# All attention ahead of the feed-forward: float32r scores on row halves, tails in quarters, the attention result kept in DRAM

## The chip, the core and the metric

The kernel runs on one core of one Trainium2 chip. A core has a matrix engine (TensorE, PE in the profile, with its weight loads listed apart as PEld), VectorE (DVE), ScalarE (ACT), GpSimd (POOL) and a queue processor (SyncE, SP) that issues transfers; POOL can issue transfers too. Each engine takes its instructions strictly in the order in which the program lists them and waits on semaphores. The metric is the device time of one execution in microseconds; less is better.

## What is computed

Sigmoid attention, and behind it a feed-forward layer with exact GELU, all in float32. Cut to what matters:

```python
q, k, v: (8, 12, 448, 64)            # batch, heads, tokens, head size
scores = q @ k.T / sqrt(64) - log(448)
x = sigmoid(scores) @ v              # laid out as (8*448 = 3584 tokens, 12*64 = 768)
h = x @ w_in                         # (768, 2048), float64 in memory
out = (0.5 * h * (1 + erf(h / sqrt(2)))) @ w_out      # (2048, 768), float64 in memory
```

There is no sum over keys in the sigmoid, so each score can be used as soon as it is there. The weights arrive as 64-bit floats, and the kernel itself makes 32-bit floats of them by integer operations ("decoding").

## The kernel before

**Two kinds of float32 product.** A float32 matmul of the source becomes two weight loads and two matrix instructions in the trace. A float32r matmul becomes one of each, but its operands carry fewer bits; where full precision is wanted, each operand is split into a float32r high part and the float32r rest, and three products (low x high, high x low, high x high) are added up in PSUM. The split is one copy on ScalarE and one subtraction on VectorE.

**The feed-forward** is written in float32r splits throughout: tokens are taken in blocks of 512, seven of them. `ffn1` (L433) makes 16 hidden tiles `ph` of 18 matmuls each (L428 to L430, six chunks of 128 channels times three products), applies GELU twice on ScalarE (L445, L446) and takes the difference on VectorE (L447). `ffn2` (L460) makes 6 output tiles `po` of 48 matmuls each (L477 to L479). So a block has 288 + 288 = 576 matmuls of 512 columns. Weights stream through `Weights`: a unit (16 "in", 12 "out") is loaded from a scratch copy in DRAM (`wst`), split into `whl` on ScalarE (L226) and VectorE (L227), and used.

**Decoding** comes first for each weight: `decoder` (L87) cuts the weights into 40 pieces (16 of 768 columns, 24 of 512), loads each as 64-bit words (`raw`, `raw_ring`, L110), and takes five VectorE and two ScalarE instructions for it (L117 to L147). What comes out is used directly for block 0 and stored in DRAM for the other blocks.

**Attention** is written in two ways. Three of the eight batches are "plain" (`scores_plain` L333, `values_plain` L349): scores and values are float32 matmuls, for two heads at once. The two heads of a pair lie on partitions 0 to 63 and 64 to 127 of `qr` and `kr`, so their score matmuls use the two row halves of the matrix engine, and the value matmuls use its two column halves. 448 keys are taken as four chunks of 128, of which the last overlaps the third by half; the overlapped rows of its probabilities are zero (`a_last`). Two plain batches run alone at the start (`attention_first` L398), 12 pairs, with the first pieces of decoding beside them, and the result goes to `xh` and `xl`. The third plain batch and the other five batches are woven into `ffn2` of the block ahead (`window` L490): a few attention instructions, then some feed-forward matmuls, and so on. The five later batches are written in float32r (`split_head`, `scores` L281, `values` L376): per head, 7 score matmuls and 7 value matmuls of 128 x 128 weights and 448 columns, with q, k, v and also the probabilities split into high and low parts. One batch (the plain one of `b == 0`) is cut into seven groups of 64 tokens through `scr_x`, and each block takes 448 tokens of one batch and 64 of that one.

What sets the order: nothing but the order in which the Python code calls the engines. `until(share)` in `window` spreads the attention evenly over a block's `ffn2`.

## Time and profile before

| what | value |
|---|---|
| median of three runs | 1220.3 us (1219.89 to 1221.09) |
| span of the profiled execution | 1224.1 us, 3.8 us over that median |
| busy share of PE, DVE, ACT, POOL | 99%, 63%, 67%, 1% |
| granted TensorE clock, mean | 0.998 |
| first score matmul, first feed-forward matmul | 4.10 us, 91.94 us |
| last block of the feed-forward, with no attention in it | 1089.72 to 1220.29 us |
| moved by DMA | 172.23 MB, mean 141 GB/s |

The span is the profiled execution's own time, from its first to its last instruction; the runs are timed apart from it. A busy share counts an instruction from its start to its modelled end, and matmuls overlap, so 99% for PE does not say that the engine had no more to give. Times within the trace count from the start of the span. "x16" in a row is a count of instructions, and the name in front of "<-" is what they write.

### The profile page before, as it was taken

What the parts mean: (1) busy time and instruction counts of PE and PEld (TensorE: products, weight loads), DVE (VectorE), ACT (ScalarE), POOL (GpSimd) and SP (SyncE); (2) the same over time, 40 slices, a digit from 0 to 9 for tenths busy, and PEclk for the clock granted to TensorE, in tenths of its full rate; (3) what the DMA queues carried; (4) which work ended last, traced back from release to release, by engine and by line L of the source; (5) the groups of instructions that cost most, each with busy time, mean ns of one, the idle gap of its engine ahead of it and who ended that gap; (6) DMA issues with size and microseconds to landing.
All of it is one profiled execution on the core that took longest, in us unless ns stands there. A gap on an engine that the chain in (4) does not pass through costs nothing.

```text
span 1224.1 us, 15057 instructions
## 1 busy us (share of the span) xinstructions
PE 1210.4 (99%) x5448; PEld 961.8 (79%) x5448; DVE 769.2 (63%) x1127; ACT 815.5 (67%) x1247; POOL 8.6 (1%) x18
## 2 busy tenths in 40 slices
PE   8999999999999999999999999999999999999998
PEld 4338866668888888888888888888888888888887
DVE  4777788623589734798445896447984378953420
ACT  7886576534699744899546997459984489954421
POOL 0000000000000000000000000000000000000000
PEclk9999999999999999999999999999999999999999
DMA  8994567524443135442244432345422544223330
GB/s 278 300 283 153 183 214 246 183 82 154 154 140 113 57 104 174 150 143 73 91 157 147 142 108 76 123 145 162 133 69 87 172 148 147 78 82 104 131 114 26
DMA packets 79881, 172.23 MB, mean 141 GB/s; under 512 B 24256, under 2 KB 39616, under 8 KB 79808
## 3 DMA queue, kind: packets, MB, share of 16 engines
q1 hardware_dynamic: 78080, 164.99, 42.4%
q0 software_dynamic: 1728, 6.29, 1.3%
q8 instruction: 43, 0.70, 0.2%
q14 instruction: 30, 0.25, 0.1%
HBM read 144.90 MB, written 26.35 MB: 140 GB/s over the span
## 4 chain that ended last, share of the span: by engine, by line
PE 95%; DMA 3%; DVE 1%; ACT 1%; SPq 0%; issue 0%; DVEq 0%; ACTq 0%
PE po L477 13%; PE po L478 13%; PE po L479 12%; PE ph L428 12%; PE ph L429 12%; PE ph L430 12%; PE pav L386 7%; PE sc L294 6%; PE pav L356 3%; PE sc L340 3%; DMA raw_ring<-w_in_dram 1%; PE sc_l L289 1%; DMA raw<-w_in_dram 1%; DMA qr<-q_dram 1%; DVE me_ring L117 0%; SPq L328 0%
## 5 line engine op out<-in xcount | busy, mean ns | idle before, releaser
L477 PE MATMUL po<-g,whl 128*128 128x512 f32 x672 | 263.3, 392 | 0.0
L478 PE MATMUL po<-g,whl 128*128 128x512 f32 x672 | 262.3, 390 | 0.0
L479 PE MATMUL po<-g,whl 128*128 128x512 f32 x672 | 261.9, 390 | 0.0
L428 PE MATMUL ph<-xh,whl 128*128 128x512 f32 x672 | 261.5, 389 | 0.0
L429 PE MATMUL ph<-xl,whl 128*128 128x512 f32 x672 | 261.4, 389 | 0.0
L430 PE MATMUL ph<-xh,whl 128*128 128x512 f32 x672 | 261.4, 389 | 0.0
L227 DVE TENSOR_TENSOR whl<-wst,whl 128x768 fp32r<-128x768 f32 (+1 forms) x168 | 179.6, 1072 | 65.1 <-ACT whl L226 61.9
L447 DVE TENSOR_TENSOR g<-gf,g 128x512 fp32r<-128x512 f32 x112 | 77.5, 692 | 212.0 <-ACT g L446 211.8
L445 ACT ACTIVATE gf<-ph 128x512 f32<-128x512 f32 x112 | 66.9, 597 | 199.4 <-PE ph L430 185.5
L226 ACT CAST whl<-wst 128x768 fp32r<-128x768 f32 (+1 forms) x168 | 155.4, 928 | 5.5 <-PE po L479 4.2
L477 PEld LDWEIGHTS po<-g,whl 128*128 128x128 f32 x672 | 126.2, 188 | 31.9 <-issue 8.1
L428 PEld LDWEIGHTS ph<-xh,whl 128*128 128x128 f32 x672 | 126.1, 188 | 26.9 <-issue 0.7
L479 PEld LDWEIGHTS po<-g,whl 128*128 128x128 f32 x672 | 126.1, 188 | 26.8
L430 PEld LDWEIGHTS ph<-xh,whl 128*128 128x128 f32 x672 | 126.1, 188 | 26.2
L429 PEld LDWEIGHTS ph<-xl,whl 128*128 128x128 f32 x672 | 126.1, 188 | 26.1
L478 PEld LDWEIGHTS po<-g,whl 128*128 128x128 f32 x672 | 126.2, 188 | 23.8
L314 ACT ACTIVATE a<-sc 128x896 f32<-128x896 f32 (+1 forms) x174 | 128.3, 786 | 17.3 <-PE sc L340 8.3
L308 DVE TENSOR_TENSOR al<-a,ah 128x896 fp32r<-128x896 f32 x120 | 97.8, 855 | 35.4 <-ACT ah L307 35.4
L307 ACT CAST ah<-a 128x896 fp32r<-128x896 f32 x120 | 85.7, 754 | 5.6 <-PE pav L386 4.2
L386 PE MATMUL pav<-ah,vs 128*128 128x448 f32 x240 | 87.7, 365 | 0.0
L294 PE MATMUL sc<-qs,ks 128*128 128x448 f32 x360 | 82.9, 366 | 0.0
L294 PEld LDWEIGHTS sc<-qs,ks 128*128 128x128 f32 x360 | 67.6, 188 | 6.8
(60 smaller groups left out, 1210.4 us busy)
## 6 DMA issues: line engine op xcount, KB each, us to landing
wst<-scr_in SPq DMA_DIRECT2D x96, 384.0 KB, 3.1
wst<-scr_out SPq DMA_DIRECT2D x72, 512.0 KB, 3.3
kr<-k_dram SPq DMA_DIRECT2D x30, 448.0 KB, 4.3
vr<-v_dram SPq DMA_DIRECT2D x48, 256.0 KB, 4.6
out_dram<-ob SPq DMA_DIRECT2D x42, 224.0 KB, 2.0
raw_ring<-w_in_dram SPq DMA_DIRECT2D x11, 768.0 KB, 7.0
raw_ring<-w_out_dram SPq DMA_DIRECT2D x16, 512.0 KB, 4.7
qr<-q_dram SPq DMA_DIRECT2D x36, 224.0 KB, 3.2
```

What stands on the lines that cost most here:

```text
L226: nc.scalar.copy(hl[:, 0, :w], t[:, :w])
L227: nc.vector.tensor_tensor(hl[:, 1, :w], t[:, :w], hl[:, 0, :w], op=ALU.subtract)
L294: nc.tensor.matmul(o, ks[:, keys], qs, start=n == 0, stop=n == 1)
L308: nc.vector.tensor_tensor(al[t][:, c], a[t][:, c], ah[t][:, c], op=ALU.subtract)
L314: nc.scalar.activation(a, sc, AF.Sigmoid, bias=NEG_LOG_S, scale=SCALE)
L386: nc.tensor.matmul(pav[:, :S], vs[:, j, c], a, start=n == 0, stop=n == len(terms) - 1)
L428: nc.tensor.matmul(ph, wl, xh[:, cc], start=cc == 0, stop=False)
L429: nc.tensor.matmul(ph, wh, xl[:, cc], start=False, stop=False)
L430: nc.tensor.matmul(ph, wh, xh[:, cc], start=False, stop=cc == NC - 1)
L477: nc.tensor.matmul(po, wl, g[fc][:, 0], start=first, stop=False)
L478: nc.tensor.matmul(po, wh, g[fc][:, 1], start=False, stop=False)
L479: nc.tensor.matmul(po, wh, g[fc][:, 0], start=False, stop=last)
```

## The change

**All attention is done first**, in one loop over 24 units (8 batches times 3); a unit is two pairs of heads, p = 0 and p = 1. There is no attention in the feed-forward any more, and no pair is woven into `ffn2`.

**Scores** (`scores`): for each pair and each of the three full chunks of 128 keys, q and k are split into `hi` and `lo` (`split`: the copy for p = 0 on ScalarE, for p = 1 on VectorE, both subtractions on VectorE), and three float32r products are added up, each for the two heads on the two row halves: 36 matmuls a unit. **The tail** of 64 keys is no longer an overlapped chunk: the tails of all four heads of a unit are four float32 matmuls of 64 x 64 weights, one on each quarter of the matrix engine (`QUARTERS`), and one sigmoid takes them all. **Values** stay float32 on column halves (`values`), 12 a unit, plus four quarters for the tail (`values_tail`). They are taken one unit later than the scores.

**The result** of a unit is copied from PSUM by VectorE and parked by POOL in `scr_x`, a DRAM buffer for all 3584 tokens, in float32 (`park`). Each block loads its 512 tokens from there (`load_x`) and splits them (`split_x`), in the middle of `ffn2` of the block ahead.

**Decoding** runs beside attention, one piece a unit up to 20 pieces (`AHEAD`), and the other 20 beside the first block. Every decoded unit is now stored to DRAM by POOL and loaded again, block 0 too. `raw` has three buffers of its own. Weights are split four units ahead everywhere.

The diff, cut to its core ("..." marks what is left out):

```diff
+    T = 512
+    NT = B * S // T
...
-    scr_x = tc.dram_tile([2, P, NPAIR, S], F32, name="scr_x")
+    scr_x = tc.dram_tile([P, NPAIR, B * S], F32, name="scr_x")
...
+    WHL, WST = 4, 3
...
-        raw_ring = sb.tile([P, 2, 2 * SUB], U32, tag="raw", name="raw_ring", bufs=1)
...
+                raw = sb.tile([P, 2 * SUB], U32, tag="raw", name=f"raw{i}", bufs=3)[:, : 2 * w]
...
+            if c0 + w == width(kind):
+                nc.gpsimd.dma_start(scratch(kind, u), self.out[:, : width(kind)])
+                self.done += 1
...
+        def to(self, chunks):
+            while self.taken < 1 + 2 * chunks:
+                next(self.steps, None)
+                self.taken += 1
...
+    AHEAD = 20
...
+                    dec.units(i + 1)
...
+            self.prepare_to(i + WHL)
...
-    def scores(b, h):
...
-            for n, lows in enumerate((0, S + TAIL)):
-                keys = slice(lows + c * P, lows + c * P + P)
-                nc.tensor.matmul(o, ks[:, keys], qs, start=n == 0, stop=n == 1)
...
+    def load_x(t):
+        nc.sync.dma_start(xl.bitcast(F32), scr_x[:, :, t * T : (t + 1) * T])
+    def split_x():
+        half = NPAIR // 2
+        for h in slice(0, half), slice(half, NPAIR):
+            nc.scalar.copy(xh[:, h], xl[:, h].bitcast(F32))
+            nc.vector.tensor_tensor(xl[:, h], xl[:, h].bitcast(F32), xh[:, h], op=ALU.subtract)
+    def attention(at, ps_sc, ps_av):
+        raws, vals, parts, probs, pavs, xs = {}, {}, {}, {}, {}, {}
+        total = B * NU
+        def load(u):
+            if u >= total:
+                return
+            b, n = divmod(u, NU)
+            raw = at.tile([P, 2, 2, S], F32, tag="qk", name=f"qk{u}", bufs=3)
+            pairs = (slice(0, 1), slice(1, 2)) if u == 0 else (slice(0, 2),)
+            for ps in pairs:
+                hps = slice(2 * n + ps.start, 2 * n + ps.stop)
+                nc.sync.dma_start(raw[:, ps, 0], q[b, hps].rearrange("p r s -> r p s"))
+                for j in range(2):
+                    src = k[b, hps, rows(j), j].rearrange("p r s -> r p s")
+                    nc.sync.dma_start(raw[rows(j), ps, 1], src)
+            raws[u] = raw
+        def load_v(u):
+            if u >= total:
+                return
+            b, n = divmod(u, NU)
+            vr = at.tile([P, 2, 2, FULL + 1, D], F32, tag="v", name=f"v{u}", bufs=3)
+            src = v[b, 2 * n : 2 * n + 2].rearrange("p r j c d -> r p j c d")
+            nc.sync.dma_start(vr, src)
+            vals[u] = vr
+        def split(u, p):
+            if u >= total:
+                return
+            raw = raws[u][:, p]
+            hi, lo = (
+                at.tile([P, 2, S], F32R, tag=x, name=f"{x}{u}_{p}", bufs=3) for x in ("hi", "lo")
+            )
+            parts[u, p] = hi, lo
+            if p == 0:
+                nc.scalar.copy(hi, raw)
+            else:
+                nc.vector.tensor_copy(hi, raw)
+            nc.vector.tensor_tensor(lo, raw, hi, op=ALU.subtract)
+        def sigmoid(u, p, c, sc):
+            a = at.tile([P, 2, S], F32, tag="a", name=f"a{u}_{p}_{c}", bufs=11)
+            nc.scalar.activation(a, sc, AF.Sigmoid, bias=NEG_LOG_S, scale=SCALE)
+            probs[u, p, c] = a
+        def scores(u, p, c):
+            if u >= total:
+                return
+            hi, lo = parts[u, p]
+            sc = ps_sc.tile([P, 2, 512], F32, tag="sc", name=f"sc{u}_{p}_{c}")[:, :, :S]
+            keys = slice(c * P, c * P + P)
+            terms = ((hi, lo), (lo, hi), (hi, hi))
+            for n, (ks, qs) in enumerate(terms):
+                for j in range(2):
+                    nc.tensor.matmul(
+                        sc[:, j], ks[rows(j), 1, keys], qs[rows(j), 0], start=n == 0, stop=n == 2
+                    )
+            sigmoid(u, p, c, sc)
+        QUARTERS = ((0, 0), (1, 1), (0, 1), (1, 0))
+        def scores_tail(u):
+            if u >= total:
+                return
+            raw = raws.pop(u)
+            sc = ps_sc.tile([P, 2, 512], F32, tag="sc", name=f"sc{u}_t")[:, :, :S]
+            for p, j in QUARTERS:
                 nc.tensor.matmul(
-                    pav[rows(j), :S], vr[:, j, c], a[:, j], start=c == 0, stop=c == 3
+                    sc[rows(p), j],
+                    raw[rows(j), p, 1, FULL * P :],
+                    raw[rows(j), p, 0],
+                    start=True,
+                    stop=True,
                 )
...
+            sigmoid(u, 0, FULL, sc)
+        def bank(u, p):
+            if (u, p) not in pavs:
+                pavs[u, p] = ps_av.tile([P, 512], F32, tag=f"pav{p}", name=f"pav{u}_{p}")
+            return pavs[u, p][:, :S]
+        def values(u, p):
+            if u < 0:
+                return
+            pav = bank(u, p)
+            for c in range(FULL):
+                a = probs.pop((u, p, c))
+                for j in range(2):
+                    nc.tensor.matmul(
+                        pav[rows(j)],
+                        vals[u][:, p, j, c],
+                        a[:, j],
+                        start=p == 0 and c == 0,
+                        stop=p == 1 and c == FULL - 1,
+                    )
+        def values_tail(u):
+            if u < 0:
+                return
+            a = probs.pop((u, 0, FULL))
+            for p, j in QUARTERS:
+                nc.tensor.matmul(
+                    bank(u, p)[rows(j)],
+                    vals[u][rows(p), p, j, FULL],
+                    a[rows(p), j],
+                    start=p == 1,
+                    stop=p == 0,
+                )
+        def park(u, p):
+            if u < 0:
+                return
+            if p == 0:
+                xs[u] = at.tile([P, 2, S], F32, tag="x", name=f"x{u}", bufs=2)
+            nc.vector.tensor_copy(xs[u][:, p], bank(u, p))
+            if p == 1:
+                b, n = divmod(u, NU)
+                nc.gpsimd.dma_start(scr_x[:, 2 * n : 2 * n + 2, b * S : (b + 1) * S], xs.pop(u))
+        load(0)
+        split(0, 0)
+        split(0, 1)
+        load(1)
+        load_v(0)
+        dec.to(-0.25)
+        load_v(1)
+        load(2)
+        for u in range(total + 1):
+            dec.to(min(u + 0.5, AHEAD) if u > 0 else 0)
+            for c in range(FULL):
+                scores(u, 0, c)
+            values(u - 1, 0)
+            split(u + 1, 0)
+            split(u + 1, 1)
+            for c in range(FULL):
+                scores(u, 1, c)
+            scores_tail(u)
+            load(u + 3)
+            values_tail(u - 1)
+            dec.to(min(u + 1, AHEAD))
+            park(u - 1, 0)
+            values(u - 1, 1)
+            park(u - 1, 1)
+            load_v(u + 2)
+            if u == total - 2:
+                load_x(0)
+                W.load_to(2)
+            if u == total - 1:
+                split_x()
+                W.prepare_to(2)
...
+                hl = W.get((t, "in", fc))
...
+                if t == 0:
+                    dec.to(AHEAD + 10 * (fc + 1) / NF)
...
+                    hl = W.get((t, "out", 2 * e + half))
+                    if t == 0:
+                        dec.to(AHEAD + 10 + 2 * e + half + 1)
+                    if e == 1 and half == 0 and t + 1 < NT:
+                        load_x(t + 1)
+                    if e == 2 and half == 0 and t + 1 < NT:
+                        split_x()
...
+        for t in range(NT):
+            ffn2(t, ffn1(t))
...
-        attention_first()
...
-        ffn1(0)
-        window(2, 0)
...
+    with tc.tile_pool(name="at", bufs=1) as at:
+        with psum("ps_sc", 3) as ps_sc, psum("ps_av", 1) as ps_av:
+            attention(at, ps_sc, ps_av)
+    ff = ctx.enter_context(tc.tile_pool(name="ff", bufs=1))
+    ps_f = ctx.enter_context(psum("ps_f", 4))
+    feed_forward(ff, ps_f)```

How the order moves, at three places. First PE in the attention: before, one plain pair in the stage that runs alone, its scores and then the values of the pair before it (`sc_0` to `sc_3` are the four chunks, `pav` the sum over them, `x2` the two heads):

```order
L340 MATMUL sc_0_237<-qk_125 128x448 x2
L340 MATMUL sc_1_242<-qk_125 128x448 x2
L340 MATMUL sc_2_250<-qk_125 128x448 x2
L340 MATMUL sc_3_255<-qk_125 128x448 x2
L356 MATMUL pav_266<-a_0_184,vr_104 64x448 x2
L356 MATMUL pav_266<-a_1_195,vr_104 64x448 x2
L356 MATMUL pav_266<-a_2_200,vr_104 64x448 x2
L356 MATMUL pav_266<-a_last_73,vr_104 64x448 x2
```

And now, a part of one unit (in `sc_1_2`, p = 1 and chunk 2; `sc_t` are the four tails; `pav_0` and `pav_1` belong to the unit before):

```order
L264 MATMUL sc_1_2_266<-lo_1_147,hi_1_146 128x448 x2
L264 MATMUL sc_1_2_266<-hi_1_146,lo_1_147 128x448 x2
L264 MATMUL sc_1_2_266<-hi_1_146 128x448 x2
L277 MATMUL sc_t<-qk_97 64x448 x4
L311 MATMUL pav_0_233<-a_0_3_182,v_101 64x448
L311 MATMUL pav_1_287<-a_0_3_182,v_101 64x448
L311 MATMUL pav_0_233<-a_0_3_182,v_101 64x448
L311 MATMUL pav_1_287<-a_0_3_182,v_101 64x448
L298 MATMUL pav_1_287<-a_1_0_157,v_101 64x448 x2
L298 MATMUL pav_1_287<-a_1_1_166,v_101 64x448 x2
L298 MATMUL pav_1_287<-a_1_2_175,v_101 64x448 x2
L264 MATMUL sc_0_0_315<-lo_0_241,hi_0_240 128x448 x2
```

One score tile takes three pairs of matmuls instead of one, the fourth chunk has become a quarter step for four heads, and the kind of use of the matrix engine (row halves, quarters, column halves) changes five times a unit.

Second, ScalarE at the same place. Before, one plain pair (`me_ring` is decoding, `xh` the copy of the result):

```order
L314 ACTIVATE a_0_240<-sc_0_237 128x896
L314 ACTIVATE a_1_245<-sc_1_242 128x896
L314 ACTIVATE a_2_253<-sc_2_250 128x896
L314 ACTIVATE a_last_74<-sc_3_255 64x896
L130 ACTIVATE me_ring<-me_ring 128x768
L133 ACTIVATE me_ring<-me_ring 128x768
L365 CAST xh_2_275<-pav_266 128x448
```

And now, one unit, that is two pairs (`hi_0` is the high part of q and k for the next unit):

```order
L252 ACTIVATE a_0_0_540<-sc_0_0_533 128x896
L252 ACTIVATE a_0_1_549<-sc_0_1_542 128x896
L252 ACTIVATE a_0_2_558<-sc_0_2_551 128x896
L245 CAST hi_0_567<-qk_391 128x896
L252 ACTIVATE a_1_0_582<-sc_1_0_575 128x896
L252 ACTIVATE a_1_1_591<-sc_1_1_584 128x896
L252 ACTIVATE a_1_2_600<-sc_1_2_593 128x896
L252 ACTIVATE a_0_3_607<-sc_t 128x896
L110 ACTIVATE me_529<-me_529 128x768
L113 ACTIVATE me_529<-me_529 128x768
```

Seven sigmoids stand where two plain pairs had eight, the copies of the result are gone from ScalarE, a copy of q and k has come, and there is one piece of decoding per two pairs instead of one per pair.

Third, PE where attention and feed-forward meet. Before, in a block of `ffn2` with one of the later batches (`sc_3_l` and `sc_3_0` are the scores of a head, `po` the feed-forward):

```order
L477 MATMUL po_1_2656<-g_6_2173,whl_2468 128x512
L478 MATMUL po_1_2656<-g_6_2173,whl_2468 128x512
L479 MATMUL po_1_2656<-g_6_2173,whl_2468 128x512
L289 MATMUL sc_3_l<-qs_3_2551,ks_3_2554 128x448
L294 MATMUL sc_3_0_2699<-qs_3_2551,ks_3_2554 128x448 x2
L294 MATMUL sc_3_1_2700<-qs_3_2551,ks_3_2554 128x448 x4
L477 MATMUL po_1_2656<-g_7_2208,whl_2468 128x512
```

And now, the only place where they meet, at the end of the last unit:

```order
L298 MATMUL pav_1_2655<-a_1_1_2600,v_2452 64x448 x2
L298 MATMUL pav_1_2655<-a_1_2_2609,v_2452 64x448 x2
L370 MATMUL ph_0_2678<-xh,whl_2637 128x512
L371 MATMUL ph_0_2678<-xl,whl_2637 128x512
L372 MATMUL ph_0_2678<-xh,whl_2637 128x512
```

From there on the list holds `ph` and `po` matmuls alone, 4032 of them, as many as before.

463 lines of the change are left out of this document (96 added, 367 removed).

## Prediction

> **What bounds the kernel now.** I read the chain of work that ended last first, then its pieces in order of time.
>
> ```profile
> PE 95%; DMA 3%; DVE 1%; ACT 1%; SPq 0%; issue 0%; DVEq 0%; ACTq 0%
> 27.06 3.16 PE pav L356 x16
> 30.22 3.21 PE sc L340 x16
> ...
> 330.57 1.22 PE sc L294 x6
> 340.71 1.42 PE pav L386 x7
> ```
>
> 95% of the path is matmul time, so the time is read as a sum over matmuls. A piece's length there goes to the start of the next, so it is time used up and not the modelled end: a plain pair costs 3.21 us for its scores and 3.16 us for its values, and a float32r matmul of 448 columns costs 1.22 / 6 = 0.203 us.
>
> Next the timeline at the two ends, and the busy time in two windows, the first stage and the last block, which is feed-forward alone.
>
> ```profile
> 4.10 8.71 PE L340 MATMUL sc<-qk 64*128 64x448 f32 x32 [4.10 <-DMA qk<-k_dram]
> 91.94 0.50 PE L428 MATMUL ph<-xh,whl 128*128 128x512 f32 x1
> 1089.72 0.39 PE L428 MATMUL ph<-xh,whl 128*128 128x512 f32 x1
> 1220.06 0.39 PE L479 MATMUL po<-g,whl 128*128 128x512 f32 x1
> 1220.53 0.59 ACT L482 COPY ob<-po 128x512 f32<-128x512 f32 x1 [10.33 <-PE po L479]
> ...
> 4.10:91.94 87.84, 81.87 (x385) 33.57 (x385) 59.46 (x81) 71.34 (x89) 0.00 (x0) 0.98 0.93 294
> 1089.72:1220.29 130.57, 130.57 (x577) 107.92 (x575) 38.76 (x42) 43.65 (x65) 0.00 (x0) 1.00 0.30 97
> ```
>
> (A window's columns are its length, busy time of PE, PEld, DVE, ACT and POOL with counts, the granted clock, the DMA share, GB/s.) The last block's 576 matmuls of 512 columns take 1220.06 - 1089.72 = 130.34 us over 575 steps, 0.2267 us each, 130.6 us a block. Seven blocks are 914.0 us. The end behind the last matmul is 1224.1 - 1220.3 = 3.8 us, the start 4.1 us. What is left, 1224.1 - 914.0 - 3.8 - 4.1 = 302.2 us, is what attention costs today: 87.8 us in the first stage, 214.4 us woven into the blocks. The first stage's 12 pairs need 12 x 6.37 = 76.4 us of PE; the other 11 us are waits at a DMA share of 0.93.
>
> **What stays.** The change issues the same 4032 feed-forward matmuls in the same form: 914.0 us, if nothing is late. So it is decided by what 24 units cost.
>
> **A unit on PE.** The rows of the weight loads of a plain pair, and of the two kinds of score matmul (count, shortest/median/longest ns), tell how half-array matmuls run.
>
> ```profile
> 31.00 0.19 PEld L340 LDWEIGHTS sc<-qk 64*128 64x128 f32 x2 [0.18 <-issue]
> 31.38 0.19 PEld L340 LDWEIGHTS sc<-qk 64*128 64x128 f32 x2 [0.18 <-issue]
> ...
> 33.78 0.14 PEld L356 LDWEIGHTS pav<-a,vr 128*64 128x64 f32 x2 [0.23 <-issue]
> ...
> 35.66 0.14 PEld L356 LDWEIGHTS pav<-a_last,vr 128*64 128x64 f32 x2 [0.23 <-issue]
> ...
> L294 PE MATMUL sc<-qs,ks x360: 362/365/369, 330.4 to 1078.5; 128*128 128x448 f32 x180
> L340 PE MATMUL sc<-qk x192: 536/536/1112, 4.1 to 230.4; 64*128 64x448 f32 x192
> ```
>
> Two loads, one for each row half, take 0.19 us together and come every 0.38 us; those of the column halves come every (35.66 - 33.78) / 5 = 0.376 us. So halves run side by side, and a float32 matmul costs 2 x 0.376 = 0.752 us for two heads. A float32 instruction lasts 536 - 365 = 171 ns longer than a float32r one of as many columns, so I take it that it streams its columns twice and float32r once.
>
> *Scores, 18 pairs of float32r on row halves a unit.* The trace has none. From below a pair costs half of 0.376 = 0.188 us; from above 2 x 0.203 = 0.406 us, if halves do not run side by side in this type. I take 0.203: same type, columns and weight width, and two loads side by side took no longer (0.19) than one. 18 x 0.203 = 3.65 us. *Values:* 6 pairs x 0.752 = 4.51 us, seen today. *Tails, two steps of four quarters:* from below 0.752 us a step, all four side by side; if only two are, 1.504. I take 0.752, since halves of rows and halves of columns each ran side by side: 1.50 us. *Changes of form:* today's pair has two, and 3.21 + 3.16 is 6.37 where 16 steps of 0.376 are 6.02, so 0.18 us each; five a unit are 0.89 us. Sum 3.65 + 4.51 + 1.50 + 0.89 = 10.55 us, and 24 units 253.2 us (2 pairs today: 12.7 us in the first stage, and 302.2 / 24 = 12.6 us on average).
>
> **What must hide beside it.** The rows by form for ScalarE, VectorE:
>
> ```profile
> L314 ACT ACTIVATE a<-sc 128x896 f32<-128x896 f32 x114 | 102.3, 918 | 17.3 <-PE sc L340 8.3 <-PE sc L294 7.8
> L307 ACT CAST ah<-a 128x896 fp32r<-128x896 f32 x60 | 56.7, 945 | 1.4
> L308 DVE TENSOR_TENSOR al<-a,ah 128x896 fp32r<-128x896 f32 x60 | 65.4, 1090 | 35.2 <-ACT ah L307 35.2
> L277 DVE CAST vs<-vr 128x512 fp32r<-128x512 f32 x30 | 12.6, 421 | 0.0
> L393 DVE TENSOR_TENSOR x<-pav,x 64x448 f32<-64x448 f32 x60 | 37.3, 622 | 12.5 <-ACT x L392 10.9
> ...
> L130 ACT ACTIVATE me_ring<-me_ring 128x768 f32<-128x768 int32 x14 | 11.9, 847 | 6.0 <-DVE me_ring L117 6.0
> ```
>
> ScalarE: 7 x 0.918 + 0.945 + 2 x 0.847 = 9.06 us a unit, below 10.55. VectorE: two subtractions 2.18, the copy of 896 at most 0.421 x 896 / 512 = 0.74, two copies out of PSUM at most 2 x 0.62 (nearest row, L393), and a piece of decoding at most 59.46 / 14 = 4.25 (busy time of the first window over its 14 pieces): 8.4 us. Both fit, ScalarE with 1.5 us to spare. On PE the scores of three chunks take 1.83 us and their sigmoids 2.75 us; three PSUM buffers and the value step of 2.3 us behind each group give ScalarE the time to catch up. Were that cover gone, PE would lose 0.9 us a group.
>
> *Transfers.* Sizes as the trace has them:
>
> ```profile
> raw_ring<-w_in_dram SPq DMA_DIRECT2D x7, 768.0 KB, 7.0
> vr<-v_dram SPq DMA_DIRECT2D x10, 256.0 KB, 5.7
> qk<-q_dram SPq DMA_DIRECT2D x6, 224.0 KB, 6.1
> qk<-k_dram SPq DMA_DIRECT2D x12, 112.0 KB, 5.9
> scr_in<-w_in SPq DMA_DIRECT2D x2, 384.0 KB, 5.2
> ```
>
> A unit loads 448 KB of q, 448 of k, 512 of v and, for the first 16 units, 768 of weights; POOL stores 384 KB of weights and 448 KB of result: 3008 KB, 3.08 MB. At 10.55 us that is 292 GB/s, just what moved at a share of 0.93 (294). So the transfers fit by a hair. POOL issues its two stores a unit behind VectorE's copies, with nothing else in its queue. SP's queue carries no stores in this stage, each load is issued two units ahead, and what waits at its head (a `raw` load for its buffer) holds q, k and v behind it. VectorE works in order: a late piece holds up the next unit's `lo`, and so its scores. Such waits stand in today's first stage:
>
> ```profile
> 59.69 7.77 DMA raw_ring<-w_in_dram
> ...
> DVE me_ring L117 <- DMA raw_ring<-w_in_dram: 20.2, 7, 11.0
> ```
>
> There the loads run one or two pieces ahead, here three. I put 3 us for one such wait not covered (0 to 20 in the range).
>
> **Start, meeting point, first block.** The first scores now wait for a copy and a subtraction: 4.10 + 0.945 + 1.09 = 6.1 us. The first unit has no values beside it, so ScalarE sets it: 7.4 us (7 x 0.918 + 0.945) against 4.6 us on PE, 2.8 us lost; its loads are the kernel's first, so I take 4. At the meeting point x and two weight units are split while the last values run, nothing is added. Block 0 decodes 20 pieces beside it; the window over today's first `ffn1` says what such work leaves:
>
> ```profile
> 92.00:157.00 65.00, 65.00 (x289) 53.84 (x288) 47.11 (x68) 38.35 (x61) 1.20 (x2) 1.00 0.49 173
> ```
>
> PE was never idle there, with VectorE at 47 of 65 us. For the block now: 38.8 us of VectorE work as in the last block, and 20 x 4.25 = 85 at most, 124 of 130.6 us. With weights split four units (about 20 us) ahead I add nothing.
>
> **Sum, against the profiled execution:** 6.1 + 4 + 253.2 + 3 + 914.0 + 3.8 = 1184.1 us, where today's is 1224.1. The median of the runs shown lies 3.8 us under that span, so 1180.3: **1180 us**, 3.3% less.
>
> **Rivals.** *A, transfers, VectorE or ScalarE set the pace of a unit.* For it: ScalarE was busy 71.34 of 87.84 us (81%) in the first stage, where waits bind; at that share 9.06 us become 11.2. At the first 30 us' 275 GB/s 3.08 MB take 11.2 too.
>
> ```profile
> 0.00:30.00 30.00, 25.06 (x112) 12.38 (x112) 13.18 (x20) 22.77 (x28) 1.83 (x6) 1.00 0.86 275
> ```
>
> Against it: loads go further ahead than today, and 11.2 is 0.65 us over 10.55. Price: 0.65 to 1.5 us in the 20 units with decoding, 13 to 30 us: 1193 to 1210. The Trainium skill (TensorEngine Tiling (Array Packing), PSUM Bottleneck) warns of it: tiling speeds up TensorE and not the emptying of PSUM. The trace agrees as far as 0.918 us a sigmoid tile is more than the 0.61 us of its matmuls.
>
> *B, only two quarters run side by side.* Nothing in the trace speaks of quarters. Price 2 x 0.752 = 1.50 us a unit, 36 us: 1216.
>
> *C, slower: float32r does not pair up on row halves.* The mechanism: the loads of the next pair are not covered by the matmuls of the one before it on the same halves. A pair then costs a load (0.19) and a stream (0.188), 0.376 instead of 0.203, 18 x 24 x 0.173 = 75 us: 1255; wholly one behind the other (0.406) 88 us: 1268. It decides from 0.296 a pair on, where the 40 us are gone. For it: a float32r stream is only half as long as today's, about as long as the load itself. Against it: in the rows at 31.00 and 31.38 both loads lie wholly inside the period of the pair before, on the same halves. The Trainium skill states a rule that would bring C about (TensorE: Matmul & The Clock Gate, Part 3, The mechanism): weight loads overlap matmuls in flight only when their row group differs. By that rule today's float32 pair would cost 0.188 us more a step than it does, so this trace disagrees.
>
> *D, nothing is gained:* the attention's own matmuls fall short, but block 0 stalls on decoded weights, each 4 to 8 us late. From 8 us on it would show; 40 us would take most of the 12 "out" units. That ends at 1190 to 1220.
>
> **How the numbers follow.** My forecast, 1170 to 1192 (0.188 a pair would give 6 us back, no start loss 4), 0.64; A 0.14; B 0.07; C 0.11; D 0.04. The range runs from 1170 up through A to 1213; outside it lie B, C and the tails of the forecast, two in ten. A measurement of this kernel tells 0.2%, 2.4 us, from no change. Faster: the forecast, A, and most of B and D (0.09), 0.87, less 0.02 for mishaps not listed: 0.85. Same 0.04, from B and D. Slower 0.11, C.
>
> **What would show it.** First feed-forward matmul near 270 us (267 without the 3 us wait), 914 us from there to the last one. Units 10.5 us apart on PE; a score tile of six matmuls in 0.61 us, the four quarters in 0.75 us. A shows as PE waiting for ScalarE or `lo`, a unit of 11.2 or more. B shows in L277 and L311, 1.5 us a step. C shows in L264, 1.1 us or more a tile. D shows as gaps among `ph` or `po` of the first block. The forecast is wrong if the attention ends before 255 us or after 285.

## The result, and the profile after

| | before | after |
|---|---|---|
| median of four runs | 1220.69 us (1219.89 to 1225.80) | 1191.85 us (1189.64 to 1194.36) |
| ratio after / before | | 0.9753, 95% interval 0.9729 to 0.9776 |
| profiled execution: its time, its span | the long run of the four, 1225.80; 1224.1 | 1189.64; 1187.9 |
| first feed-forward matmul | 91.94 us | 266.63 us |

The change makes the kernel 28.8 us faster. The prediction was 1180 us, 12 us too low, within its range of 1170 to 1213.

The timeline of TensorE after the change: start, length, line, operation, tiles, count, and in brackets the idle time before and what ended it. First the start, a unit of the steady part, and the two ends of the feed-forward:

```profile
6.82 0.74 PE L264 MATMUL sc<-lo,hi 64*128 64x448 f32 x2 [6.82 <-DVE lo L248]
...
9.97 0.56 PE L264 MATMUL sc<-hi 64*128 64x448 f32 x2
10.34 0.39 PE L264 MATMUL sc<-lo,hi 64*128 64x448 f32 x2
...
13.19 1.08 PE L277 MATMUL sc_t<-qk 64*64 64x448 f32 x8 [0.77 <-ACT a L252]
...
24.27 1.77 PE L277 MATMUL sc_t<-qk 64*64 64x448 f32 x8 [3.36 <-ACT a L252]
...
27.47 2.48 PE L298 MATMUL pav<-a,v 128*64 128x448 f32 x12
...
35.45 0.36 PE L264 MATMUL sc<-hi 64*128 64x448 f32 x2
35.65 0.36 PE L264 MATMUL sc<-lo,hi 64*128 64x448 f32 x2
...
36.34 0.98 PE L277 MATMUL sc_t<-qk 64*64 64x448 f32 x8
37.15 0.93 PE L311 MATMUL pav<-a,v 64*64 64x448 f32 x8
38.01 2.48 PE L298 MATMUL pav<-a,v 128*64 128x448 f32 x12
...
266.63 0.50 PE L370 MATMUL ph<-xh,whl 128*128 128x512 f32 x1
...
387.77 0.50 PE L398 MATMUL po<-g,whl 128*128 128x512 f32 x1 [0.73 <-DVE whl L185]
...
395.18 0.50 PE L398 MATMUL po<-g,whl 128*128 128x512 f32 x1 [1.68 <-DVE whl L185]
...
1183.89 0.39 PE L400 MATMUL po<-g,whl 128*128 128x512 f32 x1
```

A pair of float32r scores goes every 0.20 us (35.45, 35.65), eight score quarters take 37.15 - 36.34 = 0.81 us, eight value quarters with the change of form behind them 0.86 us. From the tails of the third unit on every unit is 10.51 us long, from tail to tail, and TensorE does not wait in any of them. Four waits stand in the rows above, beside the one before the first score: 0.77 us in the first unit's tails, 3.36 us in the second unit's, and 0.73 and 1.68 us in the first feed-forward block, where `po` waits for split weights. The first nine pairs of scores take 10.34 - 6.82 = 3.52 us, nearly twice their later pace.

The last steps of the chain behind each of the two places, first the start; for block 0, VectorE's and POOL's rows of the timeline stand ahead of the chain's:

```profile
10.51 11.94 DMA qk<-k_dram
...
22.47 0.94 ACT hi L245
23.41 0.83 ACT a L252
...
385.03 0.69 DVE L124 SCALAR_TENSOR_TENSOR wd_out<-me 128x512 f32<-128x512 uint32 x1
386.01 0.53 POOL L128 DMA_DIRECT2D scr_out<-wd_out  x1 [6.90 <-DVE wd_out L124]
...
386.01 2.89 DMA scr_out<-wd_out
...
388.93 3.88 DMA wst<-scr_out
...
392.82 1.06 ACT whl L184
...
393.90 1.24 DVE whl L185
```

At the start, k of the third unit arrives at 22.45 us. ScalarE had its cast of it (L245) at the head of its queue, and the sigmoids of the unit then running stood behind. TensorE ran out of free score buffers. In block 0 VectorE ends the decoding of the last weight unit at 385.72 us (L124). From there its store, its reload and its split, which ends just before 395.18 us, take 9.5 us. POOL had waited 6.90 us for VectorE before it could issue that store. So half of the 20 us of lead goes to the way through DRAM and the split, and the rest was gone before, since the decoding ended late.

The longest wait costs more than its 3.36 us. In busy time by windows (columns as in the prediction), the granted clock, third from the end, is 0.50 behind it:

```profile
20.90:24.27 3.37, 0.01 (x2) 0.00 (x0) 1.18 (x2) 1.80 (x3) 0.00 (x0) 0.97 1.07 260
24.27:27.47 3.20, 3.19 (x17) 0.80 (x17) 1.89 (x3) 2.93 (x4) 0.00 (x0) 0.50 1.06 347
```

The 16 quarters take 27.47 - 24.27 = 3.20 us there and 38.01 - 36.34 = 1.67 us a unit later: 1.5 us more.

### The profile page after: what moved, and what is told of

It is laid out like the page before. It is cut to its first block, busy times and chain, and to the rows that moved or that the text cites. A ratio compares the mean times of both kernels' runs of the same rounds, so it can differ in the third digit from the quotient of the medians.

```text
span 1187.9 us, 14649 instructions
## 1 busy us (share of the span) xinstructions
PE 1170.8 (99%) x5856; PEld 884.8 (74%) x5856; DVE 528.1 (44%) x643; ACT 547.5 (46%) x751; POOL 36.0 (3%) x56
## 4 chain that ended last, share of the span: by engine, by line
PE 81%; issue 15%; DMA 2%; POOL 1%; SPq 0%; ACT 0%; DVE 0%; POOLq 0%; ACTq 0%
PE po L398 11%; PE po L399 11%; PE po L400 11%; PE ph L370 11%; PE ph L371 11%; PE ph L372 11%; PE pav L298 7%; PE sc L264 5%; DMA qk<-k_dram 1%; PE sc_t L277 1%; PE pav L311 1%; POOL scr_out L128 0%; POOL scr_x L327 0%; DMA wst<-scr_out 0%; DMA scr_out<-wd_out 0%
## 5 line engine op out<-in xcount | busy, mean ns | idle before, releaser
L185 DVE TENSOR_TENSOR whl<-wst,whl 128x768 fp32r<-128x768 f32 (+1 forms) x196 | 210.0, 1072 | 299.3 <-ACT whl L184 296.5
L398 PE MATMUL po<-g,whl 128*128 128x512 f32 x672 | 261.8, 390 | 2.5 <-DVE whl L185 2.4
L370 PE MATMUL ph<-xh,whl 128*128 128x512 f32 x672 | 261.5, 389 | 0.0
L400 PE MATMUL po<-g,whl 128*128 128x512 f32 x672 | 261.4, 389 | 0.0
L399 PE MATMUL po<-g,whl 128*128 128x512 f32 x672 | 261.4, 389 | 0.0
L372 PE MATMUL ph<-xh,whl 128*128 128x512 f32 x672 | 261.4, 389 | 0.0
L371 PE MATMUL ph<-xl,whl 128*128 128x512 f32 x672 | 261.4, 389 | 0.0
L184 ACT CAST whl<-wst 128x768 fp32r<-128x768 f32 (+1 forms) x196 | 181.7, 928 | 140.5 <-PE po L400 117.2
L252 ACT ACTIVATE a<-sc 128x896 f32<-128x896 f32 x144 | 121.9, 919 | 59.9 <-PE sc L264 59.9
L398 PEld LDWEIGHTS po<-g,whl 128*128 128x128 f32 x672 | 126.1, 188 | 29.9 <-DVE whl L185 3.8
L370 PEld LDWEIGHTS ph<-xh,whl 128*128 128x128 f32 x672 | 126.1, 188 | 26.9 <-DVE whl L185 0.7
L372 PEld LDWEIGHTS ph<-xh,whl 128*128 128x128 f32 x672 | 126.1, 188 | 26.3
L400 PEld LDWEIGHTS po<-g,whl 128*128 128x128 f32 x672 | 126.1, 188 | 26.3
L371 PEld LDWEIGHTS ph<-xl,whl 128*128 128x128 f32 x672 | 126.1, 188 | 26.1
L298 PE MATMUL pav<-a,v 128*64 128x448 f32 x576 | 118.6, 547 | 0.0
L402 ACT COPY ob<-po 128x512 f32<-128x512 f32 x42 | 24.7, 587 | 172.5 <-PE po L400 170.9
L298 PEld LDWEIGHTS pav<-a,v 128*64 128x64 f32 x576 | 37.2, 136 | 69.7 <-issue 69.7
L376 ACT ACTIVATE g<-ph 128x512 fp32r<-128x512 f32 x112 | 66.4, 593 | 0.0
L264 PE MATMUL sc<-lo,hi 64*128 64x448 f32 x288 | 58.4, 402 | 6.8 <-DVE lo L248 6.8
```

What stands on the lines that cost most here:

```text
L184: nc.scalar.copy(hl[:, 0, :w], t[:, :w])
L185: nc.vector.tensor_tensor(hl[:, 1, :w], t[:, :w], hl[:, 0, :w], op=ALU.subtract)
L252: nc.scalar.activation(a, sc, AF.Sigmoid, bias=NEG_LOG_S, scale=SCALE)
L264: nc.tensor.matmul(sc[:, j], ks[rows(j), 1, keys], qs[rows(j), 0], start=n == 0, stop=n == 2)
L298: nc.tensor.matmul(pav[rows(j)], vals[u][:, p, j, c], a[:, j], start=p == 0 and c == 0, stop=p == 1 and c == FULL - 1,)
L370: nc.tensor.matmul(ph, wl, xh[:, cc], start=cc == 0, stop=False)
```

## The experiments

All medians below are of executions timed beside the kernel before on the same chip, and a ratio is to that. There were three chips, on which the kernel before took 1222.61 us (control to both), 1221.28 us (late_dec, f32_start, same_half, more_dma2) and 1220.79 us (f32scores, unpaired, more_dma, before2), so medians of different groups are compared with 1 to 2 us of doubt. "First `ph`" is the first feed-forward matmul, "feed-forward" the time from it to the start of the last matmul, both of the profiled execution.

| run | median us | ratio, 95% | a unit | first `ph` | feed-forward |
|---|---|---|---|---|---|
| control (after, unaltered) | 1191.60 | 0.9741, 0.9721 to 0.9760 | 10.51 | 267.76 | 919.42 |
| ahead24 | 1188.15 | 0.9718, 0.9695 to 0.9740 | 10.51 | 267.39 | 913.82 |
| early_qk | 1190.07 | 0.9730, 0.9710 to 0.9749 | 10.51 | 265.31 | 917.45 |
| both | 1185.91 | 0.9698, 0.9678 to 0.9717 | 10.51 | 266.59 | 913.83 |
| late_dec | 1182.39 | 0.9681, 0.9655 to 0.9707 | 10.51 | 262.10 | 914.50 |
| f32_start | 1181.46 | 0.9673, 0.9648 to 0.9698 | 10.51 | 261.21 | 914.38 |
| f32scores | 1204.58 | 0.9866, 0.9847 to 0.9884 | 11.39 | 280.44 | 920.10 |
| unpaired | 1192.42 | 0.9763, 0.9745 to 0.9781 | 10.52 | 269.12 | 919.86 |
| more_dma | 1195.77 | 0.9790, 0.9772 to 0.9807 | 10.51 | 272.35 | 917.92 |
| same_half | 1281.80, one run | | 14.23 | 359.20 | 916.84 |
| more_dma2 | 1200.22, one run | | 10.51, four longer | 276.07 | 917.76 |
| before2 (before, unaltered) | 1219.76, one run | | | 85.77 | 1128.12 |

### The kernels unaltered

> The changed kernel once more, unaltered, as what the next three are compared with, since its four runs so far spread from 1189.6 to 1194.4 us. Expected 1189 to 1195 us, a unit of attention of 10.5 us on PE, the same wait of 3.4 us before the second unit's tails and 3 us of gaps among the po matmuls of block 0. If the spread comes from block 0's waits on decoded weights, those gaps differ here; if it comes from the start, the wait before the tails does.

Measured: 1191.60 us (1189.78 to 1192.94 in five runs); its profiled run, 1192.94 us, has the same units, and longer waits at both places (4.48 us at the start; 0.89 and 2.12 us in block 0, with a stretch at half clock behind the latter). So the two places make the whole difference of 3.3 us between the two profiled executions (1.1 us ahead of the first `ph`, 2.2 us in the feed-forward); the spread of the runs without a trace is likely theirs too, but not shown.

> The kernel before, profiled once more. The profile that the sum was made against had a span of 1224.1 us, while the runs lay at 1219.9 to 1221.1. If that execution was a long one of its kind, this span is 1217 to 1220 us, and the difference shows in the first stage, where DMA is busy 0.93 and PE waits (first feed-forward matmul at 87 to 89 us instead of 91.9). If the span of a profile is longer than the timed run by 3 to 4 us as a rule, it is 1223 to 1225 again, with the first stage as it was.

Measured: 1219.76 us at a span of 1218.0. Its TensorE timeline, at the places where the first stage waits, and its window over that stage:

```profile
25.55 1.02 PE L340 MATMUL sc<-qk 64*128 64x448 f32 x4 [0.45 <-ACT a L314]
...
51.73 1.02 PE L340 MATMUL sc<-qk 64*128 64x448 f32 x4 [0.46 <-ACT a L314]
...
78.65 1.02 PE L340 MATMUL sc<-qr,kr 64*128 64x448 f32 x4 [1.18 <-ACT a L314]
...
85.77 0.50 PE L428 MATMUL ph<-xh,whl 128*128 128x512 f32 x1
...
4.10:85.77 81.67, 79.58 (x385) 32.80 (x385) 59.75 (x81) 71.12 (x89) 0.00 (x0) 1.00 0.96 311
```

The same places in the profile that the prediction was made from:

```profile
54.04 1.02 PE L340 MATMUL sc<-qk 64*128 64x448 f32 x4 [2.27 <-ACT a L314]
...
83.17 1.74 PE L340 MATMUL sc<-qr,kr 64*128 64x448 f32 x4 [2.35 <-ACT a L314]
84.84 3.41 PE L356 MATMUL pav<-a,vr 128*64 128x448 f32 x12
```

The first stage ends at 85.77 us here and at 91.94 us there, and from that point on both take the same 1128.12 us. So all of the 6.1 us between the two spans lie in the first stage, which has the same matmuls in both: TensorE is idle for 2.09 us here (81.67 - 79.58) and for 5.97 us there (87.84 - 81.87), and there it also ran at half clock for a while (the values at 84.84 take 3.41 us instead of 2.48). And a run's time is its span plus 1.8 us here (1219.76 - 1218.0), plus 1.7 us after the change (1189.64 - 1187.9). No run here has a time less than 1.7 us over its span.

### 24 pieces of weights decoded beside the attention, not 20

```diff
-    AHEAD = 20
+    AHEAD = 24
```

> 24 pieces of weights are decoded beside the attention instead of 20, 16 beside block 0. Theory (block 0 loses its time to the round trip of decoded weights, store and load): the three gaps of 3.0 us together go, units 20 to 23 stay at 10.5 us, so 3 us less than the unaltered kernel. Rival (the last units have no room for decoding, ScalarE or transfers bind): those four units grow to 11 us or more and the gain is eaten up, 0 to 3 us slower.

Measured: 1188.15 us, 3.5 us under the control, ratio intervals overlapping. The trace tells them apart where the medians hardly do. The group of `po` matmuls in the answer by lines (count, busy time, mean ns, then the idle time before them), after the change over its whole span and here from 260 us on:

```profile
L398 PE MATMUL po<-g,whl 128*128 128x512 f32 x672 | 261.8, 390 | 2.5 <-DVE whl L185 2.4
```

```profile
L398 PE MATMUL po<-g,whl 128*128 128x512 f32 x672 | 261.4, 389 | 0.0
```

No wait is left, and the feed-forward takes 913.82 us instead of 917.26 and 919.42. So in block 0 the decoded weights were late, and by 3.4 us in the profiled execution. The additional decoding costs the units nothing: they stay at 10.51 us.

### The third unit's q and k ahead of the weights

```diff
         load_v(0)
+        load(2)
         dec.to(-0.25)
         load_v(1)
-        load(2)
```

> At the start, q and k of unit 2 are loaded ahead of the first three weight pieces instead of behind them. Theory (the cast of unit 2 waits at the head of ScalarE's list for that load, the sigmoids of unit 1 wait behind it, PE waits for a PSUM buffer and then runs at half clock): the 3.4 us wait before the second unit's tails goes and 1.7 us of half clock with it, about 5 us less than the unaltered kernel. Rival (the start is bound by the bytes themselves): VectorE then waits for the first weight piece instead and holds up unit 2 as long, 0 to 1 us less.

Measured: 1190.07 us, 1.5 us under the control (the ranges, 1188.51 to 1190.88 and 1189.78 to 1192.94, overlap). Of the 5 us expected most did not come: the wait at the tails shrank, and another stood up, nearly as the expectation's rival has it. TensorE's row and the chain that leads to it:

```profile
21.23 0.47 PE L264 MATMUL sc<-lo,hi 64*128 64x448 f32 x2 [2.44 <-ACT a L252]
```

```profile
8.61 9.42 DMA raw<-w_in_dram
...
18.06 0.57 DVE me L99
...
18.65 0.85 ACT me L110
...
20.28 2.52 ACT a L252 x3
```

What had been late was q and k; now it is the first piece of weights (18.03 us), since all share the same first 20 us of transfers. VectorE waits for it, ScalarE's conversion waits for VectorE, and the sigmoids wait behind ScalarE's conversion. In either order TensorE waits for a load that stands far back in the queue.

### The two together

> Both of these edits. If the two losses are apart, as the theory has it, the gains add up: about 8 us less than the unaltered kernel, 1181 to 1186 us, and the attention at 10.5 us a unit throughout.

Measured: 1185.91 us, 5.7 us under the control, where about 8 were expected. By the medians 3.5 of them are block 0's, as in ahead24, and 2.2 come on top. The trace shows the gain in the feed-forward (913.83 us), but none at the start: the first `ph` comes at 266.59 us, and at 266.63 after the change. 2.75 us of wait for the first piece of weights (it lands at 18.96 us), with half clock behind it, are left there. What the start gave is so not shown by this run.

### Decoding one unit later

From "both", every point at which decoding is advanced is put a unit later, and the first pieces of weights are loaded behind the second unit's v:

```diff
-        dec.to(-0.25)
         load_v(1)
+        dec.to(-0.25)
         for u in range(total + 1):
-            dec.to(min(u + 0.5, AHEAD) if u > 0 else 0)
+            dec.to(min(u - 0.5, AHEAD) if u > 1 else 0)
...
-            dec.to(min(u + 1, AHEAD))
+            dec.to(min(u, AHEAD))
```

> The run with both edits, and decoding begins one unit later, with its first loads behind v of unit 1. Theory (what is left of the loss at the start is unit 2's split, which stands behind the first weight piece on VectorE): the 3.3 us wait at unit 2's scores goes, 2 to 3 us less than with both edits, 1182 to 1185. Rival (the start is bound by the bytes or by ScalarE): no change.

Measured: 1182.39 us (1181.61 to 1184.03 in five runs), below every run of "both" (from 1185.19); against the kernel before on the same chip it gains 38.9 us, and "both" 36.7. The tails of the first two units:

```profile
13.66 1.08 PE L277 MATMUL sc_t<-qk 64*64 64x448 f32 x8 [0.64 <-ACT a L252]
...
21.31 0.98 PE L277 MATMUL sc_t<-qk 64*64 64x448 f32 x8
```

The wait of the second unit, 2.75 us in "both" rather than the 3.3 named above, is gone, and first `ph` comes at 262.10 instead of 266.59 us. VectorE takes the first piece of weights at 21.98 us, without a wait; in "both" it stood still for it for 3.36 us, until 18.98. So the start was lost to weights that nobody needs before 260 us, ahead of q, k and v that are needed at once. The run moves their loads and their decoding together, and does not show which of the two counts for more.

### Scores of the first two units without the split

From "late_dec", units 0 and 1 take their scores in float32, one product instead of three, straight from what was loaded:

```diff
             raw = raws[u][:, p]
+            if u < 2:
+                parts[u, p] = raw, None
+                return
...
-            terms = ((hi, lo), (lo, hi), (hi, hi))
+            terms = ((hi, lo), (lo, hi), (hi, hi)) if u > 1 else ((hi, hi),)
```

> On top of that, the first two units take their scores as float32, without the split, since there PE waits for ScalarE and VectorE and not the other way round. Theory: first scores at 4.0 us instead of 6.8, two casts and six VectorE instructions less in the first 25 us, against 2 x 0.9 us more on PE: 3 to 5 us less than without it, 1178 to 1181. Rival (ScalarE's fourteen sigmoids set the start either way): 0 to 2 us less.

Measured: 1181.46 us (1180.03 to 1184.69), 0.9 us under late_dec and not told apart from it; so the rival's 0 to 2 us came, not the 3 to 5. TensorE starts 2.7 us sooner, and gives most of it back:

```profile
4.08 7.52 PE L267 MATMUL sc<-qk 64*128 64x448 f32 x24 [4.08 <-DMA qk<-k_dram]
...
30.91 0.98 PE L280 MATMUL sc_t<-qk 64*64 64x448 f32 x8 [0.56 <-ACT a L255]
```

The sooner start pushes TensorE onto ScalarE again at the third unit (0.56 us), and a float32 unit is 0.9 us longer on TensorE. It has the lowest median of all versions run: 39.8 us under the kernel before (1221.28 us in that comparison).

### Float32 scores throughout

```diff
-            parts[u, p] = hi, lo
-            if p == 0:
-                nc.scalar.copy(hi, raw)
-            else:
-                nc.vector.tensor_copy(hi, raw)
-            nc.vector.tensor_tensor(lo, raw, hi, op=ALU.subtract)
+            parts[u, p] = raws[u][:, p], None
...
-            for n, (ks, qs) in enumerate(terms):
...
+            for j in range(2):
+                nc.tensor.matmul(sc[:, j], hi[rows(j), 1, keys], hi[rows(j), 0], start=True, stop=True)
```

> The full chunks' scores as float32 matmuls of q and k as loaded, without the high and low parts: two matmuls a tile instead of six, and a unit loses one cast on ScalarE (0.94 us) and three instructions on VectorE (2.8 us). Theory (PE's own steps set the pace): a tile takes 0.75 us instead of 0.61, 6 x 0.14 = 0.86 us more a unit, 21 us more in all. Rival (ScalarE, VectorE or transfers set the pace at 10.5 us a unit): the lighter lists help or nothing changes, at most 5 us more.

Measured: 1204.58 us, 13.0 us over the control, which ran on another chip (by the gains over the kernel before, 16.2 and 31.0 us, it is 14.8); a unit is 11.39 us, 0.88 more. A group of scores and of values on the timeline:

```profile
104.06 2.53 PE L254 MATMUL sc<-qk 64*128 64x448 f32 x12
106.51 2.48 PE L286 MATMUL pav<-a,v 128*64 128x448 f32 x12
108.92 2.53 PE L254 MATMUL sc<-qk 64*128 64x448 f32 x12
```

Three chunks of two heads, two instructions for each float32 matmul, go in 106.51 - 104.06 = 2.45 us, change of form included; nine float32r pairs with theirs take 2.03 us in after (40.41 to 42.44 us). ScalarE and VectorE are freed of two casts and two subtractions a unit, and the unit became longer by what its matmuls did: TensorE sets the pace of a unit, neither of the others. The total lost less than 24 x 0.88 = 21 us because the start was shorter, as in f32_start: the first `ph` comes 13.8 us later than in after.

### Are the halves paired by the order of the list?

The three products of one head, then the three of the other:

```diff
-            for n, (ks, qs) in enumerate(terms):
-                for j in range(2):
+            for j in range(2):
+                for n, (ks, qs) in enumerate(terms):
```

> The six score matmuls of a tile in another order: first the three of one head (one row half), then the three of the other. Nothing else differs. If float32r matmuls run side by side only where they lie on different row halves, each tile now has four steps instead of three (the last of one half beside the first of the other): 0.81 us instead of 0.61, 6 x 0.20 us a unit, 29 us more in all, about 1220. If a half-array float32r matmul takes half the time whatever its neighbour is, nothing changes.

Measured: 1192.42 us, a unit of 10.52 us: nothing changed. The 29 us of the first theory did not come. The list of the built program has the six in the new order (three of one half, then three of the other):

```
320 L264 MATMUL sc7_0_0_860<-lo7_0_786,hi7_0_785 128x448
321 L264 MATMUL sc7_0_0_860<-hi7_0_785,lo7_0_786 128x448
322 L264 MATMUL sc7_0_0_860<-hi7_0_785 128x448
323 L264 MATMUL sc7_0_0_860<-lo7_0_786,hi7_0_785 128x448
324 L264 MATMUL sc7_0_0_860<-hi7_0_785,lo7_0_786 128x448
325 L264 MATMUL sc7_0_0_860<-hi7_0_785 128x448
```

and the timeline has them by twos, first product with first product, as before:

```profile
99.97 0.36 PE L264 MATMUL sc<-hi,lo 64*128 64x448 f32 x2
100.16 0.37 PE L264 MATMUL sc<-hi 64*128 64x448 f32 x2
100.36 0.38 PE L264 MATMUL sc<-lo,hi 64*128 64x448 f32 x2
```

The two of a row start 10 ns apart (100.164 and 100.174 us for the second). If the engine was handed them in the order of the list, a matmul for a free row half went ahead of two that stand before it and were waiting for the other half; then TensorE does not take its matmuls strictly in the listed order, as the part ahead of the prediction says of every engine. The rows of the trace carry no place in the list, so a new order on the way from the list to the engine is not excluded.

### Both heads on one row half

```diff
-                        sc[:, j], ks[rows(j), 1, keys], qs[rows(j), 0], start=n == 0, stop=n == 2
+                        sc[:, j], ks[rows(0), 1, keys], qs[rows(0), 0], start=n == 0, stop=n == 2
```

> All six score matmuls of a tile are put on row half 0: the second head's scores are computed from the first head's q and k, so half of the scores are left out of the computation. Counts, shapes, transfers, ScalarE and VectorE are unchanged. Theory (two float32r matmuls run side by side because they lie on different row halves): a tile takes 6 x 0.203 = 1.22 us instead of 0.61, 3.65 us more a unit, 88 us more in all, about 1279. Rival (a half-array matmul of 448 columns costs 0.1 us wherever it lies, or the engine moves one of them to the free half): no change, 1189 to 1195.

Measured: 1281.80 us, 90 us over after; a unit is 14.23 us, 3.72 more (this kernel leaves out the second head's scores and takes the first head's in their place). The pairs, which went every 0.20 us, now start 0.42 us apart (0.41 on average, (3.65 + 3.72) / 18):

```profile
104.31 0.57 PE L264 MATMUL sc<-hi,lo 64*128 64x448 f32 x2
104.73 0.57 PE L264 MATMUL sc<-hi 64*128 64x448 f32 x2
```

It is the row halves that give the pairing, and without them the change would have lost 60 us to the kernel before (1221.28 us on this chip).

### How near are the transfers to the pace?

Beside v, each of the first 18 units copies the same 512 KB once more into a DRAM buffer that nobody reads (more_dma), or twice (more_dma2, in which a second such line stands below):

```diff
             nc.sync.dma_start(vr, src)
+            if u < 18:
+                nc.sync.dma_start(junk[u], v[b, 2 * n : 2 * n + 2])
```

> The first 18 units each copy another 512 KB from v's memory to a DRAM buffer that nobody reads, 3.6 MB a unit instead of 3.08. If the transfers fit by a hair, as the prediction has it (313 GB/s at a busy share of 0.98 in the units from 27 to 59 us), these units go to about 11.5 us and the kernel takes 15 to 20 us more. If there is room, because loads are issued two units ahead and packets only look busy, it takes less than 4 us more.

> Twice the added transfer of the run with 512 KB: 1024 KB more in each of the first 18 units, 4.13 MB a unit, 393 GB/s at 10.51 us. If the limit lies just over the 338 GB/s that ran without a loss, these units are stretched to 11.5 to 12.2 us and 20 to 30 us are lost. If transfers still do not bind, units stay at 10.51 us and only the start gets longer, 5 to 10 us more than the unaltered kernel.

The windows over the steady part, in which the last two columns are the share of the transfer engines and what they moved, after the change, in more_dma, and in more_dma2:

```profile
45.00:195.00 150.00, 150.00 (x1094) 75.86 (x1098) 108.05 (x143) 117.59 (x143) 19.88 (x27) 1.00 0.91 289
```

```profile
45.00:195.00 150.00, 150.00 (x1090) 75.72 (x1086) 108.12 (x143) 117.17 (x144) 21.43 (x29) 1.00 1.03 335
```

```profile
45.00:195.00 150.00, 149.15 (x1084) 74.52 (x1078) 107.35 (x142) 117.82 (x143) 20.81 (x28) 1.00 1.03 373
```

At 335 GB/s every unit from the third on is still 10.51 us, not the 11.5 us of a limit just reached; at 373 GB/s the first that are longer appear, late (from the waits at 171 and 182 us on: 11.11 and 10.94 us, and two more by 0.03 and 0.04). What both runs lose, they lose nearly all in the first two units, where the copies queue up with q, k and v: in more_dma the wait at the second unit's tails is 6.83 us instead of 3.36, with half clock behind it.

```profile
28.57 1.77 PE L280 MATMUL sc_t<-qk 64*64 64x448 f32 x8 [6.83 <-ACT a L255]
```

So the transfers do not set the pace of a unit and had at least 46 GB/s to spare (335 - 289); at 84 GB/s more (373 - 289) they fall behind by the end of the stage. They do help to set the start.

## Why the prediction was right, and where it was not

The mechanism held: attention became 24 units at TensorE's own pace. By the steps of the sum, against the profiled execution of after:

| step | predicted us | measured us |
|---|---|---|
| first scores | 6.1 | 6.8 |
| fill 4, one raw wait 3 | 7.0 | 7.6 (266.63 - 6.82 - 24 x 10.51) |
| 24 units | 24 x 10.55 = 253.2 | 24 x 10.51 = 252.2 |
| feed-forward, to the start of the last matmul | 913.8 (914.0 less one step) | 917.3 |
| from there to the end of the span | 4.0 (3.8 and that step) | 4.0 |
| span | 1184.1 | 1187.9 |
| from the span to the median | -3.8 | +3.95 |
| median | 1180.3 | 1191.85 |

*The unit* was right to 0.04 us, and nearly so in its parts: nine pairs of scores with a change of form 2.03 us (9 x 0.203 + 0.18 = 2.01 was put), the score quarters 0.81 us (0.75), the value quarters with a change of form 0.86 us (0.93). f32scores and same_half confirm it by moving it: 0.88 us for six chunks in float32 against 18 pairs of float32r (6 x 0.752 - 3.65 = 0.86 by the prediction's prices), and 3.72 us for 18 pairs on one row half (18 x 0.203 = 3.65). What the quarters are worth was not run; as an estimate by the same prices, the fourth chunk of two pairs cost 4 x 0.752 = 3.0 us and costs 0.81 + 0.86 = 1.67 us now. With the 0.88 us of the scores that makes 2.2 us a unit, as much as lies between two pairs of the first stage before (2 x 6.37 = 12.74 us) and 10.51.

*The fill and the raw wait* came out right in sum (7.0 and 7.6 us) by luck. The wait was not far into the stage, where the row stands that it was taken from (59.69 us), but at the start, and it cost 3.36 us and 1.5 us of half clock, 4.9 where 3 was put. Early loads and decoding of weights are its cause: in late_dec 3.1 of the 7.6 us are left (262.10 - 6.78 - 24 x 10.51). The fill, put at 4 us, was some 2.5: 0.77 us of waiting for ScalarE, and 1.7 us because the first nine pairs took 3.52 us instead of 9 x 0.203 = 1.83. The prediction had no half clock in its sum, though its own row at 4.10 us has a slow start (32 instructions in 8.71 us, where the row at 30.22 us has 16 in 3.21). For the same reason its reading of the first stage before was too simple: "the other 11 us are waits", but TensorE was idle for 5.97 us of them, and the slow start and the 3.4 us at half clock behind 83.35 us are most of the rest.

*"With weights split four units (about 20 us) ahead I add nothing"* was wrong by 3.4 us, and ahead24 brings just that back. The step looked at VectorE's busy time (124 of 130.6 us) and at the lead on the splits. It left out that a decoded unit has to go to DRAM and back, 9.5 us from the end of its decoding to the end of its split, so that the decoding has to be done well before the block ends. It was not: the last unit was decoded at 385.72 us, and its first matmul, due at 332.04 + 11 x 5.44 = 391.9 us (the first `po`, and eleven units of 24 matmuls of 0.2267 us), came at 395.18. A busy sum does not tell that end: between 332 and 390 us VectorE waits 6.3 us for ScalarE's half of the splits and 2.7 us for a raw load, with decoding listed behind.

*The largest error, 7.8 of the 11.6 us, is the conversion from the span to the median.* The prediction subtracted 3.8 us, because the profiled span before lay that far above the median of the runs shown. But a span cannot be longer than its own execution: the profiled one was a long run, 1225.80 us, not among those shown. Its excess was waiting in today's first stage, which the change takes away in any case. Right would have been to add 1.7 us; the other 2.2 us is that the profiled run of after was the shortest of its four. In gains: 40.0 us were worked out against the long execution; from a usual one, of about 1218.9 us span (1220.69 - 1.8), 5.2 fall away, 3.8 are the span's own misses and 2.2 the short run: 28.8, as measured.

*The rivals.* A (transfers, ScalarE or VectorE set the pace) is refuted for the units: they do not move at 335 GB/s, and get longer when TensorE's work alone grows. "The transfers fit by a hair" read a share of 0.93 as nearly full. B (two quarters side by side) is refuted by the rows of L277 and L311. C does not happen, and its upper price was the right one: on one row half, two matmuls take 0.41 us (0.406 was put) and the kernel 90 us more (88 were put). D was real in kind and small in size: 3.4 us, not 4 to 8 us each for most "out" units.

## What to carry to other kernels

Ask of a profiled execution whether it is a usual one before working from its differences: a span longer than the median of the runs is a long run, and what made it long may be the very waits that the change removes. Where data goes out to memory and back, count the lead from the last instruction that makes it to the first that uses it, stores and queues included, not from busy shares. At a cold start all loads share one queue: order them by when they are needed, and put work that nobody needs for 200 us behind, also on the engines that wait for it.

## What the runs showed of the hardware

**Row halves run as streams of their own.** In unpaired, starts on the two halves are 10 ns apart though three matmuls of one half stand ahead in the list, and a unit is 10.52 us, where turns in listed order would need four steps of 0.203 us for each three. The Trainium skill (TensorE: Matmul & The Clock Gate, Part 3, The mechanism) has matmuls start and end strictly in program order; across row halves this trace disagrees, if the list's order is the one in which the engine got them.

**The share of the transfer engines does not tell what is left.** 289, 335 and 373 GB/s were moved at shares of 0.91, 1.03 and 1.03, and only the last lengthened a few units.

**A wait of 2 us can halve the clock, depending on where it falls.** In the profile before, a wait of 2.27 us (54.04) left the clock at 1.00 and one of 2.35 us (83.17) was followed by 3.3 us at 0.53:

```profile
54.04:55.00 0.96, 0.96 (x5) 0.31 (x5) 0.68 (x2) 0.96 (x2) 0.00 (x0) 1.00 1.01 420
...
83.17:86.50 3.33, 3.33 (x10) 1.02 (x12) 3.29 (x5) 3.27 (x5) 0.00 (x0) 0.53 0.92 354
```

What tells the two apart is where the wait lies. The records of the clock in the fourteen traces change only at whole steps of 3.41 us from the first change: in this one at 8.26 us, at 83.35 (22 steps on) and at 86.76; after the change at 10.39, 24.04 (4 steps on) and 27.45. From the first change to the last matmul, eleven full-clock steps hold 1.96 us or more of idle TensorE, and half clock follows each of them; it follows none with 1.68 us or less (1.96 us in unpaired, ahead of 398.68 us, and 1.68 us in after, ahead of 395.18 us, are the nearest to the border). The wait of 2.35 us lies in one step, 79.94 to 83.35. That of 2.27 us is cut at 52.63 into 0.86 and 1.41 us.

So such a wait, if most of it falls into one step, costs itself and up to 1.7 us more, half of a step, for each step at half clock behind it (one here, two in unpaired); where the steps lie differs from execution to execution (the first change is at 10.39 us in after and at 12.03 in control, the same kernel). The Trainium skill (TensorE: Matmul & The Clock Gate, Part 1, What's actually happening) puts the fall to half rate behind an idle window of about 3.4 us, in windows that run free of the kernel; the steps of 3.41 us agree with such a window, the 1.96 us of idling that were enough do not.
